# Attention backward of an adaLN block: dQ by 256-column matmuls over pairs of groups

## The chip, the core and the metric

One core of a Trainium2 chip runs the whole kernel in one launch. The metric is the device time of one execution in microseconds (us). An execution under the hardware profiler is measured besides; its trace gives the start and length of each instruction on the engines PE (TensorE), ACT (ScalarE), DVE (VectorE), POOL (GpSimd) and SP (SyncE, which here only issues transfers).

## The reference

The kernel computes the output of a transformer block (adaLN modulation, attention with 32 heads of 16 over 2048 rows, a squared-ReLU MLP) and the gradients of nine of its inputs. The part that matters here is attention:

```python
B, S, D = x.shape            # 1, 2048, 512
H = 32
Dh = D // H                  # 16
scale = Dh ** (-0.5)
scores = jnp.einsum('bhqd,bhkd->bhqk', q, k) * scale
p = _softmax(scores, axis=-1)
o = jnp.einsum('bhqk,bhkd->bhqd', p, v)
...
_out, _vjp = jax.vjp(_f, A_x, A_wqkv, A_wo, B_w1, B_b1, B_w2, B_b2, c, w_mod)
_grads = _vjp(grad_out)
```

In its backward pass the scores are made again, P = exp(scale S) (the softmax's denominators are already in the rows that stand for dO), dP = dO V^T less the row's correction, dS = P x dP, and then dV = P^T dO, dK = dS^T Q and dQ = dS K. For dQ the sum goes over the keys, so dS is needed with the keys on the partitions, that is, turned.

## The kernel before, in words

The program has a forward part, with the MLP and its backward folded in, then the attention backward (`attn_bwd`, called from `phase5`), and a last part (`phase6`) for the projections' gradients. In `attn_bwd` the order of PE, SP and POOL is the order of the code.

The loops: eight quads of heads `g`, in each two pairs of heads `jp`; a (`g`, `jp`) is called a pass here, 16 in all, counted from 0. A pass goes over four chunks `c` of 512 keys, and in a chunk over 16 blocks `ib` of 128 queries. One block for one chunk and the pass's two heads (`a` = 0, 1) is a unit. Four units are a group; a pass has 16 groups, m = 0 to 15, the kernel 256. "Even" and "odd" groups are those of even and odd m; `off(c, ib)` is true for the odd ones.

In each unit PE makes two score tiles of 128 x 512 (L1586) and, alternating with them, the two dP tiles of the unit before (L1511); the two use different halves of the array's rows. ACT takes exp of the scores into `pu` (L1589). DVE multiplies dP and `pu` into the group's `ds` tile (L1515); in odd groups ACT copies one of the eight dP tiles (L1523), and POOL does that product (L1524). Score tiles have three PSUM buffers (`stp`), dP tiles three (`dpp`), `ds` tiles three, `pu` tiles six.

dK and dV (`kv`, L1455): four matmuls of 512 columns for a unit, one on each of four strips of 32 of the array's columns, into one PSUM bank `acckv`. At a chunk's end ACT copies it into `kvT` (L1458). After a pass `turn` (L1468) transposes `kvT` in two halves of eight blocks, and ACT copies each half by two copies of 256 columns (L1472). These turns wait in the list `turnq`; one is taken ahead of each unit 3.

dQ: once a group's `ds` is complete (in unit 0 of the next group), SP issues a transposing transfer of it into a `dsT` tile (L1532): 32 blocks of 128 x 128 in odd groups, 28 in even ones. The other four blocks of an even group are transposed by PE in its unit 2 (`turn_ds`, L1545) and copied by ACT (L1546). There are four `dsT` buffers. The group then puts eight items (head `a`, key block `sub`) on the list `pendq`. An item (`dq`, L1478) is four matmuls of 128 columns, strip `i` taking query block `i` of the group, into the bank `accq`, where query block 4b + i stands at strip i, columns 128 b. In units 0 and 2 of each group four items are taken, once the list is longer than 16, so that a group's items run three groups behind it. A run of `dq` matmuls in one unit is called a dQ block here. After a pass's last item DVE scales `accq` into `dqT` (L1483), PE transposes it in four blocks (`turn_q`, L1491), and ACT copies the result into `dq_t` by one copy of 512 columns (L1492); this turn goes through `turnq` too.

Even quads have their operands in the tiles `keep` (K, its first 2048 columns of 8192) and `q0`; odd ones in tiles of their own. In the last pass `keep` is filled with the rows `xhat1` for `phase6`, one row block of 512 columns in each group. POOL issues these and the other loads, each behind a copy `tick` that reads the last `ds`.

Behind the loop the last three groups' dQ items are done, between matmuls of `phase6` (`dw_mm`, L1639) that are started there.

Of the kernel before, what the change touches and what calls it, by code (L numbers as in the profile page):

```python
# [9 lines left out]
BF16 = mybir.dt.bfloat16  # L10
F32 = mybir.dt.float32
# [8 lines left out]
P = 128  # L20
# [15 lines left out]
class Background:  # L36
# [13 lines left out]
    def next(self):  # L50
        while self.gens:
            r = next(self.gens[0], None)
            if r is not None:
                if isinstance(r, tuple):
                    self.mark = r[0]
                    self.seen.add(r[0])
                return r
            self.gens.pop(0)
        return None
# [46 lines left out]
class K:  # L106
# [1230 lines left out]
    def phase5(self):  # L1337
        S, D, NQ, ST, DT = self.S, self.D, self.NQ, self.ST, self.DT
        nc, io = self.nc, self.io
        opa = self.open_pool("p56a", bufs=1)  # L1340
        self.pup = self.open_pool("p5pu", bufs=6)
        self.dq_t = opa.tile([P, ST, D], BF16, name="dq_t")
        self.dk_t = opa.tile([P, ST, D], BF16, name="dk_t")
        self.dv_t = opa.tile([P, ST, D], BF16, name="dv_t")
        self.opa = opa
        self.junk6 = opa.tile([P, D], F32, name="junk6")
        nc.gpsimd.memset(self.dsa_part[:], 0.0)
        assert ST * self.H == D
        self.cs = [self.csq[:], self.rl[:].rearrange("p s h -> p (s h)"), self.mod_25[:, 1, :]]
        self.parts = [self.dq_t, self.dk_t, self.dv_t]  # L1350
        self.stp = self.open_pool("p5st", bufs=3, space=PSUM)
        self.dpp = self.open_pool("p5dp", bufs=3, space=PSUM)
        self.kvp = self.open_pool("p5kv", bufs=1)
        self.dsp = self.open_pool("p5ds", bufs=3)
        self.dtp = self.open_pool("p5dt", bufs=4)
        self.accp = self.open_pool("p5acc", bufs=1, space=PSUM)
        self.attn_bwd()

# [70 lines left out]
    def attn_bwd(self):  # L1429
# [8 lines left out]
        S, D, H, NQ, ST, SC = self.S, self.D, self.H, self.NQ, self.ST, self.SC  # L1438
        G = 4
        W = 4 * DH  # L1440
        dtp, kvp, stp, dpp = self.dtp, self.kvp, self.stp, self.dpp
        accp = self.accp
        acckv = accp.tile([P, 512], F32, name="acckv")
        nc.vector.memset(acckv[:], 0.0)
        accq = accp.tile([P, ST // G, P], F32, name="accq")
        masked, kvs = self.masked, self.kvs
        pend, pendq, turnq = [], [], []

        def kv(u):
            (T, g, jp, c, ib, kvT, pu, ds) = u  # L1450
# [21 lines left out]
                nc.scalar.copy(d, v[:, t, :, :, 0:DH])  # L1472

        def dq(u):
            (T, g, jp, c, ib0, a, sub, dsT) = u
            col = 32 * (2 * jp + a) - DH * a
            for i in range(G):
                nc.tensor.matmul(accq[32 * i:32 * i + 32, ib0 // G, :], lhsT=T["K"][:, 4 * c + sub, col:col + 32],  # L1478
                                 rhs=dsT[:, (i * 2 + a) * 4 + sub, :],
                                 start=(c == 0 and ib0 == 0 and a == 0 and sub == 0), stop=False,  # L1480
                                 skip_group_check=True)
            if (c, ib0, a, sub) == (SC - 1, ST - G, 1, 3):
                nc.vector.tensor_scalar(self.dqT[:], accq[:].rearrange("p b q -> p (b q)"), self.scale, None, ALU.mult)  # L1483
                turnq.append((g, jp, None, 0))

        def turn_q(g, jp):

            h0 = 4 * g + 2 * jp
            tp = stp.tile([P, ST // G, P], BF16, name="st")
            for b in range(ST // G):  # L1490
                nc.tensor.transpose(tp[:, b, :], self.dqT[:, b * P:(b + 1) * P], self.ident[:])  # L1491
            nc.scalar.copy(self.dq_t[:, :, h0 * DH:(h0 + 2) * DH], tp[:].rearrange("p b (i e) -> p (b i) e", i=G))  # L1492

        def kv_two(n=2):
            for _ in range(n):
# [21 lines left out]
        def off(c, ib):  # L1517
            return (c * SC + ib // G) % 2 == 1
# [7 lines left out]
        def dS(u):  # L1526

            (T, g, jp, c, ib, kvT, pu, dsg, i, grp) = u
            pend.append((T, g, jp, c, ib, kvT, pu, dsg[:, i]))
            if i == G - 1:  # L1530
                dsT, n = grp
                nc.sync.dma_start_transpose(dsT[:, n:, :], dsg[:].rearrange("p i a k -> p (i a k)")[:, n * P:])  # L1532
                for a in range(2):
                    for sub in range(4):
                        pendq.append((T, g, jp, c, ib - G + 1, a, sub, dsT))

        def turn_ds(dsg, grp, skip):

            dsT = dtp.tile([P, 8 * G, P], BF16, name="dsT")
            grp.extend((dsT, 0 if skip else 4))  # L1540
            if skip:
                return
            tp = stp.tile([P, 4, P], BF16, name="st")
            for b in range(4):
                nc.tensor.transpose(tp[:, b, :], dsg[:, 0, 0, b * P:(b + 1) * P], self.ident[:])  # L1545
            nc.scalar.copy(dsT[:, 0:4, :], tp[:])  # L1546

        tick = self.tick
        T = self.T0
# [1 line left out]
        for g in range(NQ):  # L1551
            for jp in range(2):
                if jp == 0:
                    if g + 1 < NQ:
                        Tn, later = self.load_group(g + 1)
                    else:
                        Tn, later = None, self.wq_pieces(1) + self.load_wmt()
                    cut = len(later) // 2 if Tn else len(later)
                    pieces = self.pair_pieces(g, 1) + later[:cut]
                    later = later[cut:]  # L1560
                elif g + 1 < NQ:
                    pieces = self.pair_pieces(g + 1, 0) + later
                else:
                    pieces = [(self.xhat1_6[:, st, :], self.xhat1_d.rearrange("(st p) d -> p st d", p=P)[:, st, :])
                              for st in range(ST)]
                kvT = kvp.tile([P, S], BF16, name="kvT")
                total = len(pieces)
                for c in range(SC):
                    c0 = 512 * c
                    for ib0 in range(0, ST, G):  # L1570
                        m = c * (ST // G) + ib0 // G
                        while pieces and (total - len(pieces)) * SC * ST <= m * G * total:
                            if last:
                                nc.gpsimd.tensor_copy(tick[:], last[7][0:1, 0, 0, 0:1])
                            nc.gpsimd.dma_start(*pieces.pop(0))
                        dsg, grp = self.dsp.tile([P, G, 2, 512], BF16, name="ds"), []
                        for i in range(G):
                            ib = ib0 + i
                            q = slice(ib * P, (ib + 1) * P)
                            if turnq and i == 3:  # L1580
                                turn(*turnq.pop(0))
                            pu = self.pup.tile([P, 2, 512], BF16, name="pu")
                            for a in range(2):
                                stt = stp.tile([P, 512], F32, name="st")
                                rs = slice(64 * jp, 64 * jp + 64)
                                nc.tensor.matmul(stt[:], lhsT=T["QT"][rs, q], rhs=masked["KT"][a][rs, c0:c0 + 512],  # L1586
                                                 start=True, stop=True)
                                held = dP(last, a) if last else None
                                nc.scalar.activation(pu[:, a, :], stt[:], ACT.Exp, scale=self.scale)  # L1589
                                if held is not None:  # L1590
                                    dP_pool(last, held)
                                if a == 0 and i % 2 == 1 and off(c, ib) and len(pend) >= 4:
                                    kv_two(1)
                            if last:
                                dS(last)
                            last = (T, g, jp, c, ib, kvT, pu, dsg, i, grp)
                            if i % 2 == 1 and len(pend) >= 4:
                                kv_two(1 if off(c, ib) else 2)
                            elif i % 2 == 0 and len(pendq) > 4 * G:
                                for _ in range(8 if len(pendq) > 6 * G else 4):  # L1600
                                    dq(pendq.pop(0))
                            if i == 2:
                                turn_ds(dsg, grp, off(c, ib))
            T = Tn
        with tc.manual_schedule(engines=ALL):
            for t in (2, 0):
# [11 lines left out]
            k0, v0, k1 = [dpp.tile([P, 512], F32, name="dp") for _ in range(3)]  # L1618
            self.dw_mm(k0, 1, 0, 0, ST // 2)
            turn(*turnq.pop(0))  # L1620
            for _ in range(2 * G):
                dq(pendq.pop(0))
            self.dw_mm(v0, 2, 0, 0, ST // 2)
            self.dw_mm(k0, 1, 0, ST // 2, ST)
            self.col_sum(1)
# [320 lines left out]
```

## Time and profile before

| | |
|---|---|
| median of 3 runs | 2516.48 us (2513.98 to 2519.32) |
| profiled execution | 2515.11 us, of this the span of the trace 2513.3 us |
| granted TensorE clock | 0.998 |
| PE busy | 2437.6 us (97%) |
| ACT busy | 2297.0 us (91%) |
| DVE busy | 1708.5 us (68%) |
| L1589 exp, 2048 | 1075.3 us together, 657 ns each |
| L1515 dS product on DVE, 1920 | 1180.5 us together, 684 ns each |
| L1478 dQ matmuls, 8192 | 105.5 and 105.2 us together (odd and even quads), 221 and 222 ns each |
| L1532 transposing transfers, 256 | 6.9 us from issue to landing, median |

"Together" is the time in which at least one instruction of the group runs; instructions of one engine overlap at their ends, so it is less than the number times the mean. A matmul's recorded end is modelled; its start is not, and distances between starts are the better measure of PE. In the windows shown below, a row has the window in us from the span's start and its length, then for PE, PEld (weight loads), DVE, ACT and POOL the busy time and the number of instructions, and at last the granted clock, the mean busy share of the DMA engines and the GB/s that they moved. In the chain of waits a row has the start and the length in us, and what the chain runs through. A row of waits has the engine, the waiting operation and line, what it waited for, then the us in total, the number of times and the longest.

### The profile page before, as it was taken

To read this page: it belongs to the slowest core of one execution; us is meant where nothing else is said; L and a number is where in the kernel's file an instruction comes from. 1 tells how busy PE (TensorE), PEld (TensorE's weight loads), DVE (VectorE), ACT (ScalarE), POOL (GpSimd) and SP (SyncE) were. 2 spreads that over 40 slices of the span, in tenths; PEclk is the share of its full clock that TensorE was granted. 3 is DMA by queue.
4 is the path that set the end of the run, shared out by engine and by line. 5 is a ranking of instruction groups with operands and counts; after the bars stand their busy time and mean duration, and the time that the engine had idled before them with its cause. 6 is when DMAs were issued, how large, how long until landed. Compare 5 with 4: busy or idle time off the path is not lost.

```text
span 2513.3 us, 76903 instructions
## 1 busy us (share of the span) xinstructions
PE 2437.6 (97%) x30791; PEld 1133.6 (45%) x30791; DVE 1708.5 (68%) x3519; ACT 2297.0 (91%) x3773; POOL 715.9 (28%) x1289
## 2 busy tenths in 40 slices
PE   8999999999999999999999999999999999999998
PEld 4555555555555554673333333333333333333343
DVE  6222323422332333677999999999999999999957
ACT  7999999999999997535999999999999999999935
POOL 2344531321131022255222222222222222222223
PEclk9999999999999999999999999999999999999999
DMA  4589661441343044699999999999999999999997
GB/s 166 135 180 206 173 117 67 112 100 45 102 118 75 24 134 134 133 203 210 233 225 218 219 228 221 228 227 219 221 221 226 227 224 219 227 224 231 237 191 205
DMA packets 1260558, 446.30 MB, mean 178 GB/s; under 512 B 1204052, under 2 KB 1228246, under 8 KB 1260198
## 3 DMA queue, kind: packets, MB, share of 16 engines
q1 hardware_dynamic: 1219654, 336.29, 71.5%
q0 software_dynamic: 38464, 104.04, 13.7%
q8 instruction: 241, 3.95, 0.6%
q10 hardware_dynamic: 2080, 1.05, 0.1%
q14 instruction: 119, 0.97, 0.1%
HBM read 75.83 MB, written 64.49 MB: 56 GB/s over the span
## 4 chain that ended last, share of the span: by engine, by line
PE 55%; ACT 24%; DMA 12%; issue 4%; DVE 3%; POOL 0%; SPq 0%; DVEq 0%; ACTq 0%; POOLq 0%
ACT pu L391 19%; PE st L1586 15%; DMA dsT<-ds 10%; PE st L388 8%; PE acckv L1455 7%; PE accq L1478 5%; ACT pu L1589 4%; PE accbank L322 3%; DVE ds L1515 2%; PE dps L1050 2%; PE pps L1237 2%; PE dp L1511 1%; PE st L1545 1%; PE dps L995 1%; PE pps L631 1%
## 5 line engine op out<-in xcount | busy, mean ns | idle before, releaser
L1515 DVE TENSOR_TENSOR ds<-dp,pu 128x512 bf16<-128x512 f32 x1920 | 1180.5, 684 | 33.2 <-PE dp L1511 26.4
L1589 ACT ACTIVATE pu<-st 128x512 bf16<-128x512 f32 x2048 | 1075.3, 657 | 34.6 <-PE st L1586 21.3
L391 ACT ACTIVATE pu<-st 128x1024 bf16<-128x1024 f32 x992 | 912.1, 1077 | 2.9 <-PE st L388 2.7
L388 PE MATMUL st<-QTm,KTq 128*128 128x512 bf16 x1984 | 587.7, 377 | 19.5 <-ACT pu L391 6.0
L322 PEld LDWEIGHTS <-pu 128*128 128x128 bf16 x8192 | 347.5, 96 | 235.7 <-issue 2.5
L1511 PE MATMUL dp<-kvm,q 64*128 64x512 bf16 x1024 | 363.5, 384 | 1.3 <-DVE g2w L1056 0.7
L1511 PE MATMUL dp<-kvm,dOTg 64*128 64x512 bf16 x1024 | 362.2, 384 | 0.0
L322 PE MATMUL accbank<-Vaug,pu 128*128 128x17 bf16 x8192 | 357.7, 171 | 1.2 <-ACT Vaug L522 0.9
L1586 PE MATMUL st<-kvm,q 64*128 64x512 bf16 x1024 | 349.9, 381 | 4.7 <-ACT pu L1589 0.2
L1586 PE MATMUL st<-kvm,QTg 64*128 64x512 bf16 x1024 | 349.4, 381 | 4.0
L388 PEld LDWEIGHTS <-KTq 128*128 128x128 bf16 x1984 | 188.1, 96 | 176.1 <-issue 124.4
L1524 POOL TENSOR_TENSOR ds<-junk,pu 128x512 bf16<-128x512 f32 x64 | 73.9, 1154 | 370.3 <-ACT junk L1523 284.1
L1455 PE MATMUL acckv<-ds,Qg 128*16 128x512 bf16 x1024 | 176.2, 382 | 0.0
L1455 PE MATMUL acckv<-pu,dOg 128*16 128x512 bf16 x1024 | 175.9, 382 | 0.0
L1455 PE MATMUL acckv<-pu,q 128*16 128x512 bf16 x1024 | 175.8, 382 | 0.0
L1455 PE MATMUL acckv<-ds,q 128*16 128x512 bf16 x1024 | 175.8, 382 | 0.0
L1524 POOL TENSOR_TENSOR ds<-csq,pu 128x512 bf16<-128x512 f32 x64 | 73.8, 1153 | 354.5 <-ACT csq L1523 354.5
L302 POOL DMA_DIRECT2D QTm<-QTq_d x124 | 63.3, 512 | 340.8 <-PE st L388 320.0
L1586 PEld LDWEIGHTS <-q 64*128 64x128 bf16 x1024 | 66.9, 93 | 141.0 <-issue 108.8
L1586 PEld LDWEIGHTS <-QTg 64*128 64x128 bf16 x1024 | 66.6, 93 | 141.0 <-issue 108.0
L329 DVE RECIPROCAL rl<-accbank 128x4 f32<-128x4 f32 x128 | 23.0, 179 | 157.4 <-PE accbank L322 157.2
L1478 PE MATMUL accq<-dsT,Kg 128*32 128x128 bf16 x4096 | 105.5, 221 | 10.5 <-DMA dsT<-ds 10.2
(387 smaller groups left out, 3168.2 us busy)
## 6 DMA issues: line engine op xcount, KB each, us to landing
KTq<-KTq_d POOLq DMA_DIRECT2D x24, 512.0 KB, 3.7
duT_d<-auT POOLq DMA_DIRECT2D x3, 1792.0 KB, 7.7
aT_d<-rT POOLq DMA_DIRECT2D x3, 1792.0 KB, 11.1
KTq_d<-KTq SPq DMA_DIRECT2D x32, 128.0 KB, 2.2
QTq_d<-ev_fm SPq DMA_DIRECT2D x32, 128.0 KB, 4.3
ktm_d<-ev_tm POOLq DMA_DIRECT2D x32, 128.0 KB, 2.6
VTq_d<-vT POOLq DMA_DIRECT2D x4, 1024.0 KB, 6.3
dsT<-ds SPq DMA_TRANSPOSE x256, 6.9
```

What stands on the lines that cost most here:

```text
L302: nc.gpsimd.dma_start(QTm[j][32 * j:32 * j + 32, :], self.QTq_d[g, 32 * j:32 * j + 32, 512 * qc:512 * (qc + 1)])
L322: nc.tensor.matmul(acc[:, a, sub, :], lhsT=pu[:, a, sub * P:(sub + 1) * P], rhs=Vaug[:, kb, h, :], start=(kb == 0 and a == 0 and sub == 0) ...
L388: nc.tensor.matmul(stt[:, a, :], lhsT=KT[:, kb * P:(kb + 1) * P], rhs=QTm[2 * jp + a][:], start=True, stop=True)
L391: nc.scalar.activation(pu[:], stt[:], ACT.Exp, scale=self.scale)
L1050: nc.tensor.matmul(pt[:], lhsT=a[st], rhs=g_tm[:, st, :], start=(st == 0), stop=(st == ST - 1))
L1455: nc.tensor.matmul(acckv[r:r + DH, :], lhsT=T[n][:, ib, col:col + DH], rhs=src[:, a, :], start=(ib == 0), stop=(ib == ST - 1))
L1478: nc.tensor.matmul(accq[32 * i:32 * i + 32, ib0 // G, :], lhsT=T["K"][:, 4 * c + sub, col:col + 32], rhs=dsT[:, (i * 2 + a) * 4 + sub, :], ...
L1511: nc.tensor.matmul(dp[:], lhsT=T["dOT"][rd, ib * P:(ib + 1) * P], rhs=masked["VT"][a][rd, 512 * c:512 * (c + 1)], start=True, stop=True)
L1515: nc.vector.tensor_tensor(dsg[:, i, a], dp[:], pu[:, a, :], ALU.mult)
L1524: nc.gpsimd.tensor_tensor(dsg[:, i, 1], f[:], pu[:, 1, :], ALU.mult)
L1586: nc.tensor.matmul(stt[:], lhsT=T["QT"][rs, q], rhs=masked["KT"][a][rs, c0:c0 + 512], start=True, stop=True)
L1589: nc.scalar.activation(pu[:, a, :], stt[:], ACT.Exp, scale=self.scale)
```

## The change

A dQ item covers two groups. It is still (`a`, `sub`), but its four matmuls have 256 columns: strip r / 32 takes two neighbouring query blocks of the first group (strips 0 and 1) or of the second (2 and 3). `accq` has the same 512 columns in another order, and `turn_q` copies its result by two copies of 256 columns. The items of a pair are put on the list when the second group's transfer has been issued, and two items are taken in each of units 0 and 2 once the list is longer than 8; in the last pass four are taken at a time. `dsT` buffers are five, handed out by a list `dT_free` and given back after a pair's last item: four in their pool and one in the last 4096 columns of `keep`, which is not used from group 3 of the last pass on. A turn of `kvT` is taken from group 2 on, that of dQ from group 7 on. Behind the loop one of the three runs of dQ items is left out, since a pair covers two groups.

```diff
-        self.dtp = self.open_pool("p5dt", bufs=4)
+        dtp = self.open_pool("p5dt", bufs=1)
+        n = 32 * P
+        self.dT_free = [dtp.tile([P, n], BF16, name=f"dsT{k}")[:] for k in range(4)] + [self.keep[:, ST * D - n:]]
...
-        accq = accp.tile([P, ST // G, P], F32, name="accq")
+        accq = accp.tile([P, 512], F32, name="accq")
...
         def dq(u):
-            (T, g, jp, c, ib0, a, sub, dsT) = u
+            (T, g, jp, c, ib0, a, sub, dsTs) = u
             col = 32 * (2 * jp + a) - DH * a
-            for i in range(G):
-                nc.tensor.matmul(accq[32 * i:32 * i + 32, ib0 // G, :], lhsT=T["K"][:, 4 * c + sub, col:col + 32],
-                                 rhs=dsT[:, (i * 2 + a) * 4 + sub, :],
+            o = 256 * (ib0 // (2 * G))
+            for r in range(0, P, 32):
+                v = dsTs[r // 64].rearrange("p (i w k) -> p i w k", i=G, k=P)
+                nc.tensor.matmul(accq[r:r + 32, o:o + 256], lhsT=T["K"][:, 4 * c + sub, col:col + 32],
+                                 rhs=v[:, r // 32 % 2 * 2:r // 32 % 2 * 2 + 2, 4 * a + sub, :],
                                  start=(c == 0 and ib0 == 0 and a == 0 and sub == 0), stop=False,
                                  skip_group_check=True)
-            if (c, ib0, a, sub) == (SC - 1, ST - G, 1, 3):
-                nc.vector.tensor_scalar(self.dqT[:], accq[:].rearrange("p b q -> p (b q)"), self.scale, None, ALU.mult)
+            if (a, sub) != (1, 3):
+                return
+            dT_free.extend(dsTs)
+            if (c, ib0) == (SC - 1, ST - 2 * G):
+                nc.vector.tensor_scalar(self.dqT[:], accq[:], self.scale, None, ALU.mult)
                 turnq.append((g, jp, None, 0))
...
-            nc.scalar.copy(self.dq_t[:, :, h0 * DH:(h0 + 2) * DH], tp[:].rearrange("p b (i e) -> p (b i) e", i=G))
+            for h in range(2):
+                nc.scalar.copy(self.dq_t[:, 8 * h:8 * h + 8, h0 * DH:(h0 + 2) * DH].rearrange("p (s i) e -> p s i e", i=2),
+                               tp[:, 2 * h:2 * h + 2, :].rearrange("p i (s e) -> p s i e", s=G))
...
                 dsT, n = grp
-                nc.sync.dma_start_transpose(dsT[:, n:, :], dsg[:].rearrange("p i a k -> p (i a k)")[:, n * P:])
-                for a in range(2):
-                    for sub in range(4):
-                        pendq.append((T, g, jp, c, ib - G + 1, a, sub, dsT))
+                nc.sync.dma_start_transpose(dsT.rearrange("p (b k) -> p b k", k=P)[:, n:, :],
+                                            dsg[:].rearrange("p i a k -> p (i a k)")[:, n * P:])
+                two.append(dsT)
+                if len(two) == 2:
+                    pendq.extend((T, g, jp, c, ib - 2 * G + 1, a, sub, two[:]) for a in range(2) for sub in range(4))
+                    two.clear()
...
-        def turn_ds(dsg, grp, skip):
-            dsT = dtp.tile([P, 8 * G, P], BF16, name="dsT")
+        def turn_ds(dsg, grp, skip, late):
+            dsT = next(t for t in dT_free if not late or t is not own)
+            dT_free[:] = [t for t in dT_free if t is not dsT]
             grp.extend((dsT, 0 if skip else 4))
...
+                end = (g, jp) == (NQ - 1, 1)
...
-                            if turnq and i == 3:
+                            if turnq and i == 3 and m >= (7 if turnq[0][2] is None else 2):
                                 turn(*turnq.pop(0))
...
-                            elif i % 2 == 0 and len(pendq) > 4 * G:
-                                for _ in range(8 if len(pendq) > 6 * G else 4):
+                            elif i % 2 == 0 and len(pendq) > 2 * G:
+                                for _ in range(4 if end else 2):
                                     dq(pendq.pop(0))
                             if i == 2:
-                                turn_ds(dsg, grp, off(c, ib))
+                                turn_ds(dsg, grp, off(c, ib), end and m > 2)
...
             turn(*turnq.pop(0))
-            for _ in range(2 * G):
-                dq(pendq.pop(0))
             self.dw_mm(v0, 2, 0, 0, ST // 2)
```

## The prediction

> **What bounds the kernel now.** I read the busy shares of the page first, then windows, the chain of waits inside one stretch, and the waits with their releasers.
>
> ```profile
> PE   8999999999999999999999999999999999999998
> DVE  6222323422332333677999999999999999999957
> ACT  7999999999999997535999999999999999999935
> ...
> L1478 PE MATMUL accq<-dsT,Kg 128*32 128x128 bf16 x4096 | 105.5, 221 | 10.5 <-DMA dsT<-ds 10.2
> ```
>
> The change touches only the attention backward, from about 1166 us (first L1589 exp) to 2388 us, 1222 us in 256 groups. There PE, DVE and ACT are all in the top tenth, so the shares don't say who leads. The windows of pass 9 go closer: its first four groups, then two stretches of four groups each.
>
> ```profile
> 1852.33:1872.50 20.17, 19.99 (x287) 7.65 (x284) 19.09 (x33) 20.10 (x43) 5.41 (x13) 1.00 1.13 229
> 1872.50:1890.90 18.40, 18.23 (x266) 6.71 (x264) 18.33 (x31) 18.36 (x38) 4.58 (x10) 1.00 1.09 213
> 1890.90:1909.31 18.41, 18.30 (x266) 6.71 (x264) 18.36 (x32) 18.36 (x38) 5.03 (x11) 1.00 1.21 234
> ```
>
> Four groups cost 18.4 us where nothing is turned, 20.2 us at a pass's start. What ACT needs at least: six exps in a row take 3.09 us with the last one's 0.66, so they start 0.49 us apart at most (0.48 in the closest pairs); 32 exps, four copies of 512 columns (0.47 to the next start) and one kvT (0.57) make 17.7 us. DVE starts its products 0.60 apart; 30 of them are 17.9 us. Both leave some 0.5 to 0.7 us of each 18.4 to waiting. The chain of waits in that stretch says for whom:
>
> ```profile
> 1902.26 0.21 PE st L1586
> 1902.47 0.00 PE dp L1511
> 1902.47 0.34 PE accq L1478 x16
> 1902.81 0.33 PE st L1545 x4
> 1903.14 0.32 PE st L1586
> 1903.46 0.00 PE dp L1511
> 1903.46 0.37 PE st L1586
> 1903.83 0.02 PE dp L1511
> 1903.85 0.54 PE acckv L1455 x8
> ```
>
> It runs on PE piece after piece; only in the second group of the four (1897.4 to 1900.0) does it go over to ACT. So PE sets the pace in about three groups of four, by under 4%. A dQ block of 16 matmuls is 0.34 us of the chain, and the chain's table puts 5% of the span on L1478. The other thing PE waits for:
>
> ```profile
> PE accq L1478 <- DMA dsT<-ds: 15.5, 30, 1.3
> ```
>
> **The change part by part. Matmuls of 256 columns.** Before, each of 505 dQ blocks in the loop is four rounds of four matmuls, one per strip. In the timeline the four of a round start 3 to 4 ns apart and the rounds 56 ns apart (1714.446, .512, .568, .624); the last round's start is 0.15 us before the next kind of matmul. So a block is 340 ns: 4 x 56 + 116. A column costs (215 - 56) / 384 = 0.41 ns, taking the step of two dK/dV rounds of 512 columns (0.54 against 0.325 us for one round) as the other end. A round of 256 is then 56 + 128 x 0.41 = 109 ns, and a block of two rounds 2 x 109 + 110 to 116 = 328 to 334 ns. The saving is 6 to 12 ns; I take 9. The number of blocks stays, except in the last pass: still one in every unit 0 and 2 of a group. Over 479 blocks that is 4.3 us of PE time, three quarters on the path: **-3.2 us** (bounds 0 and -6). In the last pass two blocks become one of four rounds, 4 x 109 + 113 = 549 instead of 680 ns, 13 times: 1.7 us; the longer burst stands before an exp's scores, so I take **-1.0** (bounds -1.7 and +1).
>
> A rule bears on this. The Trainium skill, TensorE: Matmul & The Clock Gate (section "Wait — 56ns, not 53.3ns?"), has a floor of about 25 ns from one matmul's start to the next, however small. By it the eight matmuls less per block would be worth up to 200 ns, 100 us over the kernel. The starts 3 to 4 ns apart in this trace go against it for different strips, so its price is not used. Another page, TensorEngine Tiling (Array Packing), section "Key Properties", says that changing the tiling mode drains the engine; the 0.15 us behind a block's last round, for 53 ns of its columns, fits that, and the change removes no such drain.
>
> **Pairs of groups.** Before, group n's turned dS is first used three groups later in unit 0, two groups (some 9.5 us) behind the issue of its transpose. After, the pair (2k, 2k+1) is used from group 2k+4 on: the odd group keeps exactly that lead, the even one gets one group (4.7 us) more. The waits split by place. Where the 28 blocks of an even group are late, the first matmul of the block runs (its operand came through PE) and the pause stands behind it:
>
> ```profile
> 1828.09 0.23 PE L1478 MATMUL accq<-dsT,keep 128*32 128x128 bf16 x1
> 1829.49 0.30 PE L1478 MATMUL accq<-dsT,keep 128*32 128x128 bf16 x8 [1.17 <-DMA dsT<-ds]
> ```
>
> Eight waits are of this kind: 0.55, 0.43, 0.33, 1.17, 0.19, 0.48, 0.49 and 0.39, together 4.0 us. They go. What is late next is the ds tile: with three buffers DVE's first product of group n+3 overwrites what that transpose reads, about 0.7 us behind the dQ block (the block starts at 1900.35, the next dP at 1900.69 with 0.39). Only the wait of 1.17 reaches so far, so 0.5 comes back: **-3.5** (bounds 0, if all of it comes back at the next odd group, and -4). The other 11.5 us stand on odd groups and stay. As the loop gets some 0.6% quicker, their lead of 9.5 us shrinks by 0.05 us each, over 22 waits: **+1.0** (bounds 0 and +4).
>
> **The moved turns.** The transposes of kvT leave groups 1 and 2 for 2 and 3, that of dQ leaves group 3 for 7. In pass 9 the starts of every eighth exp give groups 1, 2, 3 and 7 as 4.83, 5.05, 5.06 and 4.57 us, their unburdened likes 5, 10 and 11 as 4.30, 4.52 and 4.57. So a kvT turn costs 0.53 (its two ACT copies are 2 x 0.265) and dQ's 0.49. Group 1 gives back 0.53, group 3 pays 0.04 more, group 7 pays two copies of 256 columns, 0.53, or half of it if ACT has slack there as it has against 4.30. That is -0.23 to +0.04 per pass; over 15 passes **-1.5**, the extra ACT copy included (bounds -8, if group 7 hides it all, and +8.5, if group 1 gives nothing back). DVE's scaling of accq (0.60 to the next start) moves one group on, from an even group with eight products to an odd one with seven; I take 0, the upper bound is 0.60 in 15 passes, +9, if it was covered and no longer is. Queued behind a late turn is the next unit's score matmul, and behind that ACT's exp.
>
> **Fifth buffer.** Every buffer is released in the unit in which, or before which, it is taken again, and the SP queue gets as many transposes, in the same order, 256; POOL's queue is unchanged, though its loads of xhat1 in the last pass come to the fifth buffer's place only from group 8 on, after its last use. Nothing (0, or +1 if a load waits).
>
> **Tail.** Before, three blocks of 32 matmuls follow the loop: the middle one, with a wait of 0.39 us, takes from 2392.15 to 2393.32. After there are two of 256 columns, each 8 x (109 - 56) = 0.42 us longer: -1.17 + 0.84 = **-0.3**.
>
> Sum: -3.2 - 1.0 - 3.5 + 1.0 - 1.5 - 0.3 = -8.5 us. The profiled execution took 2515.1 us (span 2513.3 and 1.8 around it), so 2506.6 for its like; the median of the runs, 2516.5, lies 1.4 above it, and I forecast **2508 us** as their median.
>
> **The rivals.** *The odd transposes hold the pace.* The transposes fly two groups before use, and 22 odd groups already arrive late; if what PE saves returns as waiting for these, all but the turns' and a fifth of the rest goes: -0.2 x 7.7 - 1.8 + 1 = -2, **2514 us**. For it: the DMA share of the windows, above 1.0, and three quarters of the waiting on the odd groups, which the change leaves their lead. Against it: most odd groups do not wait at all.
>
> *The turns cost more where they are now: slower.* Group 3 gets the second kvT turn and, behind its last dQ block, DVE's scaling, just ahead of group 4, where DVE has eight products and PE the first pair of the new pass. If group 1 gives nothing back and group 7 pays in full, that is 0.57 a pass; if the scaling then delays group 4's products, 0.60 more: 1.17 x 15 = +17.5, and with the other terms (-7.0) +10.5, **2527 us**. It decides from 7.0 / 15 = 0.47 us a pass on. For it: groups 2 and 3 are the dearest of a pass behind its first, each with a turn. Against it: group 5, without a turn, runs at 4.30, just what ACT needs, so group 1 should too.
>
> *Instructions are the cost, not columns.* If issue rather than streaming filled the block's 187 ns, halving the matmuls would give up to 90 ns a block, 0.75 x 479 x 90 = 32 us: **2476 us**. Against it are the even steps of 56 ns and the dK/dV rounds, whose cost grows with columns.
>
> **How the numbers follow.** Forecast 0.54, DMA rival 0.26, slower turns 0.16, instructions 0.04. The forecast's own range, from its terms, is 2502 to 2513. The range 2498 to 2518 takes in the DMA rival and the turns' bound of -8, and leaves out the last rival and most of the slower one. A change below 0.2% (5 us) can't be told from none here: faster means below 2511.5. Of the forecast 0.49 lies there, with the last rival 0.53; same 0.31 (0.05 of the forecast, 0.23 of the DMA rival, 0.03 of the slower); slower 0.16, the rest of these two.
>
> **What would show it.** Right: L1478's blocks at about 0.33 us for eight matmuls; no pause inside a block behind its first matmul, and about 11 to 13 us of waits on dsT, all at the head of a block; steady stretches of four groups at 18.3 us; group 1 at 4.3 and group 7 near 5.0. Wrong: blocks well below 0.3 us, or above 0.34; waits on dsT of 20 us or more; group 1 still at 4.8.

## The result, and the profile after

The changed kernel takes 2509.89 us (median of 22 runs, 2502.91 to 2527.07); the kernel before took 2516.22 us in the 22 runs beside them (2511.31 to 2524.13). The ratio is 0.9974 [0.9963, 0.9984], 6.5 us less. The profiled execution after has a span of 2509.0 us, against 2513.3.

The page after: part 1 (PE and PEld), part 2 (the digits of DVE and ACT), a row of part 3, and part 4's shares of the chain. Beneath it, from the page of before, the same two rows of parts 3 and 4.

```profile
PE 2438.6 (97%) x26695; PEld 1080.0 (43%) x26695; DVE 1709.6 (68%) x3519; ACT 2295.0 (91%) x3789; POOL 716.4 (29%) x1289
...
DVE  6222322422332344677999999999999999999957
ACT  7999999999999997534999999999999999999935
...
q8 instruction: 209, 3.42, 0.6%
...
PE 58%; ACT 27%; DMA 7%; issue 4%; DVE 3%; POOL 1%; SPq 0%; DVEq 0%; ACTq 0%; POOLq 0%
```

```profile
q8 instruction: 241, 3.95, 0.6%
...
PE 55%; ACT 24%; DMA 12%; issue 4%; DVE 3%; POOL 0%; SPq 0%; DVEq 0%; ACTq 0%; POOLq 0%
```

PE runs 4096 matmuls less and is as busy as before (2437.6 us then). Its instructions are fetched in 209 packets of 16 KB where there were 241. The chain's DMA share fell from 12% to 7%. (These shares say little: a second profile of the changed kernel, e5 below, gives 46% for PE, 34% for ACT and 10% for DMA. Where two engines are nearly tied, the chain follows now one and now the other.)

The windows of pass 9 after, four groups each. The turns of `kvT` stand in the first row and that of dQ in the second; the last two rows have no turn, as the prediction's last two had none.

```profile
1849.97:1869.89 19.92, 19.72 (x219) 6.55 (x217) 19.27 (x33) 19.76 (x43) 5.45 (x13) 1.00 1.22 217
1869.89:1888.83 18.94, 18.68 (x206) 6.04 (x204) 18.55 (x32) 18.89 (x41) 5.06 (x11) 1.00 1.10 236
1888.83:1907.23 18.40, 18.20 (x202) 5.82 (x200) 18.21 (x31) 18.35 (x38) 4.49 (x9) 1.00 1.14 209
1907.23:1925.62 18.39, 18.28 (x201) 5.92 (x200) 18.34 (x31) 18.34 (x38) 5.03 (x11) 1.00 1.19 236
```

Four groups without a turn take 18.40 and 18.39 us, where they took 18.40 and 18.41. The first four groups are 0.25 us shorter than before (20.17) and the second four 0.54 longer (18.40): the turn of dQ moved.

Two stretches of PE's timeline after: a dQ block that runs through, then one that waits.

```profile
1890.94 0.29 PE L1484 MATMUL accq<-dsT,keep 128*32 128x256 bf16 x2
1890.95 0.28 PE L1484 MATMUL accq<-keep 128*32 128x256 bf16 x2
1891.06 0.28 PE L1484 MATMUL accq<-dsT,keep 128*32 128x256 bf16 x2
1891.07 0.28 PE L1484 MATMUL accq<-keep 128*32 128x256 bf16 x2
1891.27 0.40 PE L1559 MATMUL st<-ident,ds 128*128 128x128 bf16 x4
```

```profile
1755.56 0.29 PE L1484 MATMUL accq<-dsT,Kg 128*32 128x256 bf16 x2
1756.12 0.40 PE L1484 MATMUL accq<-dsT,Kg 128*32 128x256 bf16 x6 [0.28 <-DMA dsT<-ds]
```

Eight matmuls take 0.33 us to the next kind (1890.94 to 1891.27), in two rounds 0.12 us apart. The pause stands behind the second matmul: strips 0 and 1 read the pair's even group, strip 2 is the first that needs the odd one. All ten waits on turned dS in the loop have this form now, so no even group is late any more.

The waits on turned dS in the loop alone (1160 to 2386 us): first before, then after, where the fifth buffer shows under the name `keep`.

```profile
PE accq L1478 <- DMA dsT<-ds: 15.1, 29, 1.3
```

```profile
PE accq L1484 <- DMA dsT<-ds: 3.8, 8, 0.9
PE accq L1484 <- DMA keep<-ds: 0.9, 2, 0.5
```

From 15.1 us in 29 waits to 4.7 us in 10. The odd groups alone had 11.5 before.

### The profile page after: what moved, and what is told of

It is laid out like the page before. It is cut to its first block, busy times and chain, and to the rows that moved or that the text cites. A ratio compares the mean times of both kernels' runs of the same rounds, so it can differ in the third digit from the quotient of the medians.

```text
span 2509.0 us, 68721 instructions
## 1 busy us (share of the span) xinstructions
PE 2438.6 (97%) x26695; PEld 1080.0 (43%) x26695; DVE 1709.6 (68%) x3519; ACT 2295.0 (91%) x3789; POOL 716.4 (29%) x1289
## 4 chain that ended last, share of the span: by engine, by line
PE 58%; ACT 27%; DMA 7%; issue 4%; DVE 3%; POOL 1%; SPq 0%; DVEq 0%; ACTq 0%; POOLq 0%
ACT pu L391 18%; PE st L1601 17%; PE acckv L1459 8%; PE st L388 8%; ACT pu L1604 7%; PE accq L1484 5%; DMA dsT<-ds 3%; PE accbank L322 3%; PE dps L1050 2%; PE pps L1237 2%; PE st L1559 1%; PE dp L1522 1%; PE dp L1652 1%; DVE ds L1526 1%; DMA keep<-ds 1%
## 5 line engine op out<-in xcount | busy, mean ns | idle before, releaser
L388 PEld LDWEIGHTS <-KTq 128*128 128x128 bf16 x1984 | 188.2, 96 | 177.5 <-issue 125.6
L1601 PEld LDWEIGHTS <-q 64*128 64x128 bf16 x1024 | 66.9, 94 | 159.6 <-issue 144.0
L1522 PEld LDWEIGHTS <-q 64*128 64x128 bf16 x1024 | 89.8, 93 | 56.7 <-issue 50.4
```

Of the source, the lines that this page charges most:

```text
L388: nc.tensor.matmul(stt[:, a, :], lhsT=KT[:, kb * P:(kb + 1) * P], rhs=QTm[2 * jp + a][:], start=True, stop=True)
L1522: nc.tensor.matmul(dp[:], lhsT=T["dOT"][rd, ib * P:(ib + 1) * P], rhs=masked["VT"][a][rd, 512 * c:512 * (c + 1)], start=True, stop=True)
```

## The experiments

Three counts of mine, from the starts of instructions in each trace, run through all of them. *Loop*: from the first exp of the attention backward to the last. *Quiet pass*: for each of the 16 groups of a pass the 20th percentile of its duration over passes 1 to 14, summed; that is a pass in which nothing is late. *Waits*: the delay of dQ blocks in the loop over their usual spacing (somewhat more than the waits above, since it counts the restart too).

| kernel | ratio to before [95%] | loop, us | quiet pass, us | waits, us (number) | dQ block, ns |
|---|---|---|---|---|---|
| before | 1 | 1221.3 | 75.38 | 19.7 (43) | 340 |
| changed | 0.9974 [0.9963, 0.9984] | 1215.2 | 75.33 | 8.5 (20) | 335 |
| e1 | 0.9998 [0.9982, 1.0015] | 1222.3 | 75.37 | 14.6 (25) | 340 |
| e2 | 1.0 [0.9985, 1.0014] | 1224.2 | 75.77 | 13.0 (24) | 335 |
| e3 | 1.0015 [1.0, 1.003] | 1225.5 | 75.74 | 12.1 (28) | 340 |
| e4 | 0.9994 [0.9978, 1.001] | 1226.1 | 75.48 | 20.8 (35) | 339 |
| e5 | 0.9972 [0.9959, 0.9985] | 1217.6 | 75.34 | 11.4 (22) | 335 |
| e6 | 0.99 [0.9881, 0.9919] | 1205.4 | 75.36 | 0 | 339 |
| e7 | 0.9918 [0.99, 0.9937] | 1207.1 | 75.36 | 0 | 335 |
| e8 | 0.9933 [0.9914, 0.9952] | 1206.5 | 74.83 | 10.7 (22) | 225 |
| e9 | 1.0133 [1.011, 1.0156] | 1257.7 | 75.40 | 46.7 (61) | 335 |
| e10 | 0.9925 [0.9906, 0.9944] | 1207.8 | 75.36 | 0 | 335 |
| e11 | 0.9976 [0.9963, 0.9988] | 1217.1 | 75.76 | 1.5 (3) | 335 |
| e12 | 0.995 [0.9932, 0.9969] | 1215.1 | 75.51 | 2.5 (5) | 335 |

The ratios are medians of many runs. Loop, quiet pass and waits are of one profiled execution each, and the changed kernel's two (changed, e5) differ by 2.4 us and 2.9 us in loop and waits: smaller differences than that are not read from them. The profiled execution of e4 lies 5.3 us above e4's median.

### e1 to e4: the parts alone

e1 is the changed kernel with matmuls of 128 columns, in the same pairs of groups:

```diff
-            for r in range(0, P, 32):
-                v = dsTs[r // 64].rearrange("p (i w k) -> p i w k", i=G, k=P)
-                nc.tensor.matmul(accq[r:r + 32, o:o + 256], lhsT=T["K"][:, 4 * c + sub, col:col + 32],
-                                 rhs=v[:, r // 32 % 2 * 2:r // 32 % 2 * 2 + 2, 4 * a + sub, :],
+            for h in range(2):
+                for r in range(0, P, 32):
+                    v = dsTs[r // 64].rearrange("p (i w k) -> p i w k", i=G, k=P)
+                    nc.tensor.matmul(accq[r:r + 32, o + 128 * h:o + 128 * h + 128], lhsT=T["K"][:, 4 * c + sub, col:col + 32],
+                                     rhs=v[:, r // 32 % 2 * 2 + h, 4 * a + sub, :],
```

> The changed kernel with each 256-column dQ matmul split into two of 128 columns; pairs of groups, five buffers and late turns stay. Theory of the prediction (PE sets the pace, a block's 6 to 9 ns count): blocks back at 340 ns, 3 to 4 us slower than the changed kernel, some 3 us faster than the kernel before. Rival, from the trace of after (steady groups took the same 36.80 us for eight as before, 36.81): the columns are worth nothing, same time as the changed kernel, 6 to 7 us faster than before.

e2 is the changed kernel with its turns as early as they can be:

```diff
-                            if turnq and i == 3 and m >= (7 if turnq[0][2] is None else 2):
+                            if turnq and i == 3 and (m >= 4 or turnq[0][2] is not None):
```

> The changed kernel with the turns of kvT in groups 1 and 2 again and that of dQ in group 4. Theory of the prediction: 1.5 us slower than the changed kernel, 5 us faster than before. Rival (the late dQ turn in group 7 stretches the lead of group 5's transpose, which is first used in group 8): group 7 back to 4.57 us, waits on dsT in group 8 come back, 2 to 4 us slower than the changed kernel.

e3 is both edits together, so that the pairs alone are left of the change.

> Both at once: the changed kernel with 128-column matmuls and early turns, so that only the pairs of groups with their five buffers are left of the change. Theory of the prediction: the pairs alone are worth the 3.5 us of waits on even groups less 1 us, 2 to 3 us faster than before. Rival (the pairs and the late turns share the whole gain): 3 to 4 us faster than before; no wait on dsT at odd groups of use.

e4 is the kernel before with the changed kernel's condition on the turns.

> The kernel before with the late turns alone (kvT from group 2 on, dQ from group 7 on). Theory of the prediction: 1.5 us faster than before. Rival: the waits of group 8 on group 5's transpose go (2.1 us in the trace of before), those of group 2 grow since group 1 gets 0.53 us shorter; 1 to 3 us faster, and if the late turns alone carry the change, 6 us faster.

None of the parts alone gains anything that can be told: pairs alone 1.0015, pairs with late turns 0.9998, wide matmuls with early turns 1.0, late turns alone 0.9994. Only all three together give 0.9974 (0.9972 again in e5). So the 128 or 256 columns decide about 0.0025 of the time, 6 us, between e1 and the changed kernel, and about as much (4.5 us between the medians of e3 and e2, 2524.86 and 2520.31) with early turns. Yet the quiet pass is the same with either width: 75.37 and 75.33 us, 75.74 and 75.77. So neither expectation of e1 came: it takes the time of before. What it has more than the changed kernel is waiting; its waits on turned dS in the loop:

```profile
PE accq L1485 <- DMA dsT<-ds: 10.6, 17, 1.3
```

The pairs brought 15.1 us down to 10.6; the wide matmuls bring it to 4.7 (6.6 in e5). These are single profiles: with early turns the two widths have 7.6 us (e3) and 7.9 us (e2).

The turns show in single groups of the quiet pass (us):

| group | 1 | 2 | 3 | 4 | 7 | 8 to 15 |
|---|---|---|---|---|---|---|
| before | 4.83 | 5.05 | 5.06 | 4.98 | 4.57 | 36.81 |
| changed | 4.30 | 5.02 | 5.06 | 4.99 | 5.09 | 36.80 |
| e2 | 4.83 | 5.05 | 4.56 | 5.88 | 4.56 | 36.82 |
| e4 | 4.30 | 5.03 | 5.12 | 5.14 | 5.05 | 36.80 |

In the changed kernel group 1 gives 0.53 back and group 7 pays 0.52. But with pairs a pass's last item runs one group later, so dQ's turn can't stand in group 3 any more; taken as soon as it can be, in group 4 (e2), it costs 5.88 - 4.99 = 0.89 there, beside DVE's scaling and eight DVE products. The quiet pass of e2 is 0.44 longer than the changed kernel's, 6.6 us over 15 passes. So the late turns don't gain; they take away what the pairs would cost.

### e5 to e8: is it PE's time, or the transposes?

e5 is the changed kernel again, as the measure for this chip.

> The changed kernel once more, on one chip with the next three. All theories: 6 to 7 us faster than before.

In e6 and e7 (before, and changed) the transposing transfers leave out the last query block of each group, so that they are shorter and never late:

```diff
-                nc.sync.dma_start_transpose(dsT[:, n:, :], dsg[:].rearrange("p i a k -> p (i a k)")[:, n * P:])
+                nc.sync.dma_start_transpose(dsT[:, n:24, :], dsg[:].rearrange("p i a k -> p (i a k)")[:, n * P:24 * P])
...
-                                 rhs=dsT[:, (i * 2 + a) * 4 + sub, :],
+                                 rhs=dsT[:, (min(i, 2) * 2 + a) * 4 + sub, :],
```

> The kernel before with lighter transposes: SP's transfers leave out the last query block of each group (20 and 24 blocks of 128 x 128 in place of 28 and 32), and dQ reads the third block again in its place, so PE, ACT and DVE have the same work. It leaves out a fourth of dQ's sum. Waits of dQ on dsT should go. Theory of the prediction (the waits are 15.5 us, PE sets the pace else): 12 to 15 us faster than before. Rival (a wait is mostly made good later, since ACT and DVE have slack): under 8 us.

> The changed kernel with the same lighter transposes, likewise leaving out a fourth of dQ's sum. Theory of the prediction (columns -4.2, turns -1.5, apart from the waits): 5 to 6 us faster than the lighter kernel before. Rival (the change works only through the waits on dsT): the same as the lighter kernel before within 2 us.

e8 is the changed kernel without the dQ matmuls of every second key block:

```diff
-            for r in range(0, P, 32):
+            for r in range(0, 0 if sub % 2 else P, 32):
```

> The changed kernel without the dQ matmuls of the odd key blocks: a dQ block in the loop is one round of 256 columns, 109 ns shorter. It leaves out half of dQ's sum. Theory of the prediction (PE on the path in three groups of four): 0.75 x 480 x 0.109 = 39 us faster than the changed kernel, bounded by ACT and DVE near 25 us. Rival (ACT, DVE and the transposes hold the pace): under 8 us faster.

e6 is 23 us faster than the kernel before, more than either theory had, and 16 of them lie in the loop. Without waits on turned dS the change gains nothing: the ratios are 0.99 for e6 and 0.9918 for e7. It even costs something there, which neither expectation had: the medians are 2496.40 and 2501.06 us, and no run of e7 is as fast as the slowest of e6. Of these 4.7 us the loops show 1.7 (1205.4 and 1207.1 us), and that is the last pass (76.1 and 77.7 us), where a unit takes four items in one run. The rest lies behind the loop, 120.6 us in e6 and 125.2 in e7; that part takes 122 to 129 us in the full kernels' profiles, and why e6's is shorter is open. So all that the change gains, it gains in waits for transposes.

And PE's time is hardly on the path. The same eight steady groups, 8 to 15, of a pass of e8 (pass 11):

```profile
2034.42:2052.72 18.30, 17.88 (x170) 5.77 (x168) 18.01 (x30) 18.30 (x39) 4.47 (x9) 1.00 1.04 233
2052.72:2071.06 18.34, 18.02 (x169) 5.69 (x168) 18.34 (x31) 18.34 (x38) 5.00 (x11) 1.00 1.11 231
```

A block is 110 ns shorter (335 to 225), eight blocks 0.88 us, and four groups go from 18.40 to 18.30 and 18.34: a tenth of it arrives. PE's busy time is the one that falls (18.20 to 17.88), ACT's fills the whole window before and after. Over the run e8 is 2505.79 us against 2514.64 for e5, 8.9 us for some 480 x 0.110 = 53 us of PE time; 25 to 39 were expected if PE was on the path, under 8 if it was not.

### e9 and e10: what fewer instructions do

Between e1 and the changed kernel the block's 5 ns can't be the 6 us (480 of them are 2.4 us, and the quiet pass hardly shows them), so something else that differs is tried: the 8192 instructions (4096 matmuls, 4096 weight loads) that PE no longer has to fetch. e9 puts 8192 empty instructions into the changed kernel, on POOL, whose own time is not scarce; e10 does the same in e7, where transposes are never late.

```diff
             nc.gpsimd.tensor_tensor(dsg[:, i, 1], f[:], pu[:, 1, :], ALU.mult)
+            for _ in range(64):
+                nc.gpsimd.engine_nop()
```

> The changed kernel with 64 empty instructions on POOL behind each of its 128 dS products: 8192 instructions more to fetch, as many as the change took from PE, and no other work. Theory (instruction fetches share the transfer engines with the transposes, and the 256 columns help through fewer fetches): the transposes land 0.2 to 0.4 us later, waits on dsT 13 to 20 us instead of 8 to 11, 3 to 6 us slower than the changed kernel, that is about the time of before. Rival (what helped was PE's own time): the time of the changed kernel, 6 to 7 us faster than before.

> Control for the empty instructions: the same 8192 in the changed kernel with the lighter transposes, which leaves out a fourth of dQ's sum. If they cost only through late transposes: the time of the lighter changed kernel, 0.8% faster than before. If they cost POOL time on the path: slower than that by as much as the run without the lighter transposes.

From the page of e9: a row of part 3 (the fetches of the other engines; it was 119 packets and 0.97 MB), the shares of the chain, and a group of part 5.

```profile
q14 instruction: 183, 1.50, 0.2%
...
PE 48%; ACT 24%; DMA 18%; issue 5%; DVE 3%; POOL 1%; POOLq 0%; SPq 0%; DVEq 0%; ACTq 0%
...
L1484 PE MATMUL accq<-dsT,keep 128*32 128x256 bf16 x1632 | 108.3, 279 | 13.0 <-DMA dsT<-ds 12.8
```

The waits view of e9, whole run:

```profile
PE accq L1484 <- DMA dsT<-ds: 28.0, 34, 2.5
...
PE accq L1484 <- DMA keep<-ds: 9.5, 11, 2.2
```

The empty instructions cost 1.0133 against 0.9972, 40 us, and nothing in e10 (0.9925 against 0.9918, 64 packets more there too). The quiet pass is unchanged (75.40 us), so no engine that matters works longer; the loop is 40.1 and 42.5 us longer than in the changed kernel's two profiles, and my count of waits went up by 35 to 38. POOL's products end where they did, 4.84 us behind the odd group's first exp in the median, so `ds` is not late by them. What the empty instructions do reaches the kernel only through late transposes.

The same can be seen in the kernels themselves. I took the time from issue to landing of each transposing transfer, and counted how many instruction packets began while it flew:

| kernel | packets in the loop | transfers without a packet, of 256 | landing without: even, odd groups | with: even, odd | mean: even, odd |
|---|---|---|---|---|---|
| before | 207 | 23 | 5.58, 6.73 us | 6.90, 7.87 | 6.86, 7.80 |
| e1 | 206 | 18 | 5.86, 6.66 | 6.99, 7.92 | 6.94, 7.89 |
| changed | 175 | 59 | 5.34, 6.70 | 6.71, 7.82 | 6.47, 7.66 |
| e5 | 175 | 53 | 5.35, 6.56 | 6.90, 7.97 | 6.55, 7.71 |
| e9 | 238 | 23 | 5.58, 7.20 | 6.96, 8.49 | 6.91, 8.41 |
| e10 | 238 | 63 | 4.21, 5.68 | 5.11, 6.56 | 4.93, 6.54 |

(medians, then means.) A transfer that meets a packet lands 0.9 to 1.5 us later. Some of that is only that a longer flight meets more packets. With 31 packets less in the loop, 35 to 41 transfers more than in e1 have a free flight, and the mean landing is 0.2 to 0.5 us earlier against e1. The other full kernels keep this order: with 206 or 207 packets (before, e1, e3, e4) the means are 6.86 to 6.94 us in even and 7.80 to 7.89 in odd groups, with 174 or 175 (changed, e2, e5, e11, e12) 6.46 to 6.69 and 7.65 to 7.71, with 159 (e8) 6.38 and 7.56.

e9 does not settle by itself that the packets are the cause, since the empty instructions do a second thing. A run of 64 holds POOL for 1.3 us behind its product, and POOL also issues the loads. In the changed kernel 122 of the 251 loads in the loop are issued in the first us of an even group; in e9, and in e10, none is, and most come 2 to 3 us into it. Transfers of odd groups are slower in e9 even where they met no packet (7.20 us in the median of nine, 6.55 and 6.69 in the changed kernel's two profiles). Which part of the 40 us comes from the packets and which from the moved loads, no run tells.

The Trainium skill, Runtime: NRT & Kernel Launch (section "Instruction fetch mechanics"), says that each engine's sequencer fetches its instructions by a DMA queue of its own, in blocks of 16 KiB, and that the cost of crossing into the next block is mostly hidden. The size agrees for PE here (3.95 MB in 241 packets); POOL's 64 added packets are of 8 KB (0.53 MB), and here the measurement decides. That the cost is mostly hidden agrees for the engine that fetches: all runs of 64 empty instructions in e9 take 1.31 to 1.35 us, and e10 takes as long as e7.

### e11 and e12: more lead for the odd groups

e11 gives the pairs one group more lead, with a sixth buffer in the place of a weight tile that is needed late (its code is left out here):

```diff
-                            elif i % 2 == 0 and len(pendq) > 2 * G:
-                                for _ in range(4 if end else 2):
+                            elif i % 2 == 0 and len(pendq) > (3 * G if 16 * (2 * g + jp) + m < 16 * (2 * NQ - 3) + 8 else 2 * G):
+                                for _ in range(4 if end or (16 * (2 * g + jp) + m >= 16 * (2 * NQ - 3) + 8 and len(pendq) > 4 * G) else 2):
```

> The changed kernel with a sixth buffer of turned dS (in the place of WmT, which is loaded in the last quad) up to the middle of pass 13, and dQ items taken one group later, once the list is longer than 12: odd groups lead by three groups in place of two. Theory (waits of dQ on dsT are what is left to gain): waits on dsT gone up to pass 13, 5 to 8 us faster than the changed kernel, 12 to 15 us faster than before. Rival (a late transpose only moves its stall to the ds tile that DVE waits for): 0 to 3 us faster than the changed kernel.

e12 does so too, and takes three items instead of two in groups 2 and 3, so that a pass's last items, its scaling and its turn come where they were:

```diff
+                        lead = 16 * (2 * g + jp) + m < 16 * (2 * NQ - 3) + 8
...
+                            elif i % 2 == 0 and len(pendq) > (3 * G if lead and m not in (2, 3) else 2 * G):
+                                for _ in range(4 if end or (not lead and len(pendq) > 4 * G) else 3 if lead and m in (2, 3) else 2):
```

> The longer lead once more, but three items are taken at a time in groups 2 and 3, so that a pass's last item and DVE's scaling come in group 3 again, as in the changed kernel; group 5 then has no items. Theory (with the longer lead the waits on dsT went, and what was lost is the scaling, 0.4 us a pass in groups 4 and 5): groups 4 to 7 as in the changed kernel, waits on dsT under 3 us up to pass 13, 4 to 7 us faster than the changed kernel, 10 to 14 us faster than before. Rival (the longer bursts beside the turns cost as much as the scaling did): the time of the changed kernel.

The waits of e11 in its whole run, and of e12:

```profile
PE accq L1485 <- DMA dsT<-ds: 2.1, 3, 1.3
```

```profile
PE accq L1485 <- DMA dsT<-ds: 2.1, 3, 1.1
```

The waits are all but gone, and e11 gains nothing over the changed kernel by it, where 5 to 8 us were expected. The stall has not moved to the `ds` tile: DVE waits for transfers 1.1 us in e11's loop. But its quiet pass is 75.76 us, 0.43 longer, most of it in group 5 (4.65 instead of 4.30), behind DVE's scaling that now comes in group 4. e12 puts that right in part (75.51; groups 2 and 3 are dearer by 0.10 and 0.08) and has the best ratio of all full kernels: 2510.75 us against 2521.94 beside it, 0.995 [0.9932, 0.9969]. A gain over the changed kernel is not shown by that: the intervals overlap, and e12's loop of 1215.1 us is as long as the changed kernel's 1215.2.

## Why the prediction came out right, and where it didn't

The time was right: 2509.9 us against 2508, the ratio 0.9974 against 0.9966 by the sum. The sum came to it by other terms than the runs show, so that the two meet so closely is luck: PE's time, -3.2 in the sum, gave nothing, and the waits of odd groups, +1.0 in the sum, went down by 5 to 7 us.

| term | predicted, us | shown |
|---|---|---|
| 256 columns, as PE time | -3.2 | block 335 ns, 328 to 334 worked out; steady groups 18.40 as before, so about 0. In waits the width is worth about -6 (e1 against changed) |
| larger blocks in the last pass | -1.0 | +1.6 where no transpose is late (e6, e7); 78.8 to 77.8 us with the waits in it |
| even groups' waits | -3.5 | gone, but pairs with late turns are not faster than late turns alone (e1 0.9998, e4 0.9994) |
| odd groups' waits | +1.0 | 11.5 us before, 10.6 in e1, 4.7 and 6.6 in the changed kernel |
| moved turns | -1.5 | 4.83 to 4.30 in group 1, 4.57 to 5.09 in group 7: about 0 |
| fifth buffer | 0 | its waits are 0.9 of 4.7 us, and it takes 48 of 256 transfers: no more than its share |
| tail | -0.3 | 125.6 and 125.5 us behind the last exp; 122 to 129 in other profiles of full kernels. Its wait on turned dS, 0.4 us before, is 2.5 us after, which the sum left out |

**The step that failed** is "So PE sets the pace in about three groups of four". It rested on two things: the chain ran on PE piece after piece, and ACT's floor, worked out from its closest pairs of exps, came to 17.7 us of 18.4. e8 refutes it: with 0.88 us less of PE time in four groups, 0.05 to 0.10 arrive. In the changed kernel itself, 16 blocks shorter by 5 ns left the eight steady groups at 36.80 us (36.81 before). The rate of the closest pairs is not reached over a group; in the window of before ACT stood idle for 0.04 of 18.40 us, DVE for 0.07 and PE for 0.17, and that line was there to read. Which of ACT and DVE holds the 18.3 us, or their buffers together, the runs don't tell; that it is not PE, they do.

**The second one** is "The other 11.5 us stand on odd groups and stay". The lead of the odd groups did stay, and with 128 columns (e1) the waits did too: 10.6 us. What changed is the other end: the transposes landed earlier (7.66 us in the mean of odd groups, 7.89 in e1), which the prediction held fixed. It went through the change instruction by instruction and never asked what fetching the instructions moves.

**The signs.** Blocks of 0.335 us, group 1 at 4.30 and group 7 at 5.09 us came as named. Steady groups stayed at 18.40 us instead of 18.3; the waits are 7.2 us over the whole run instead of 11 to 13; and in the loop they all stand behind a block's second matmul, not at its head.

**The moved turns** were given the right sizes, and the wrong comparison. Measured against the old place they are worth about nothing; measured against the place that pairs leave to dQ's turn, they are worth 6.6 us (e2).

**The rivals.** "The odd transposes hold the pace" was right that this is where the time lies: without late transposes the change gains nothing. Its price was off, since it too held the landing fixed. "The turns cost more where they are now" is refuted: groups 2, 3 and 4 cost what they did (5.02, 5.06, 4.99 us). "Instructions are the cost" named the wrong place: blocks are 335 ns, not below 300, so issue on PE is not it. Fewer instructions may still be what pays, by fewer fetches; that is likely from the landings, and not shown alone.

**What stays open.** That later transposes cost the kernel its time is shown by e6 and e7, and by e9 with e10. That instruction fetches are what delays them is not shown alone: the landings go with the number of packets in ten profiles, but e9 moves POOL's loads together with the packets. Nor is it shown that fetches are the whole of the 256 columns' 6 us. e2 and e3, with early turns, differ by 4.5 us in their medians, but one profile of each does not show it in the waits (13.0 and 12.1 us); and e8, with the fewest packets, waits no less than the changed kernel (10.7 us). 64 small packets and the moved loads cost 40 us in e9, where 32 larger packets less gained about 6; with a lead that some odd groups just miss, such a cost need not be in proportion, but no run here gives its law.

## What to carry to other kernels

Before you price an engine's saved time, take some of its work away in one run: a chain of waits that runs through one of three engines that are all busy 99% of a stretch does not say that its time is on the path. Where a transfer is used just as it lands, look at everything that moves its landing, the loads and instruction fetches that fly with it among it: empty work on an engine with time to spare cost 40 us here, and 4096 matmuls less gained 6 without any engine getting quicker. And when an operand is put off by one step, follow what comes behind its last use (here a scaling and a turn): its new place can cost as much as the change gains.

## What the hardware did that was not expected

8192 empty instructions on POOL, in 128 places where it had time, cost 40 us (1.0133 [1.011, 1.0156] against 0.9972 [0.9959, 0.9985]), nearly all of it in waits for transposing transfers, and nothing (0.9925 against 0.9918) where these had slack. They brought 64 instruction packets and pushed about half of POOL's loads back by 1 us or more; the runs do not part the two. In the loop a transposing transfer during which an instruction packet began took 6.9 us in the median of even groups, and 5.6 us where none did (before), 7.9 and 6.7 in odd ones. PE's 8192 instructions less are 32 packets of 16 KB, among 446 MB that all queues move.
